# An eight-batch linear attention and gMLP kernel on one core: a product in one bank of a PSUM pair no longer waits for an addition that reads the other bank, and the order of all steps is searched anew

## The chip, the cores and the metric

The kernel runs on one core of a Trainium2 chip. The metric is the time of the whole program on the device, in microseconds (us). The engines that matter are TensorE (PE, matrix products into PSUM), VectorE (DVE), ScalarE (ACT), GpSimd (POOL) and the queues that move data between memory and the chip.

## The reference

```python
# 8 batches, 8 heads, S = 576 positions, head size 64, model size 512
q_s = softmax(q, over the head's 64)          # 1e-9 added to each sum
k_s = softmax(k, over the 576 positions)
kv  = einsum('bhsd,bhse->bhde', k_s, v)
x   = einsum('bhsd,bhde->bhse', q_s, kv)      # then 576 x 512 per batch

h    = gelu_tanh(x @ w_in)                    # 576 x 1024
u, v = h[..., :512], h[..., 512:]
v_n  = (v - mean(v)) / sqrt(var(v) + 1e-6) * g_ln
v_s  = einsum('ts,bsd->btd', w_sg, v_n) + b_sg
out  = x + (u * v_s) @ w_out
```

All is float32.

## The kernel before, in words

**Products.** Each float32 product is made of three faster ones: an operand is cast to a reduced form `hi` (on ACT), the rest `lo` = operand − `hi` is formed by a subtraction (on DVE or POOL), and PE adds up hi·hi, hi·lo and lo·hi. A step that makes such a `lo` thus stands between the value and a third of its products.

**Steps of a batch b.** `load_q`, `load_k`, `load_v`; the two softmaxes (`q_…`, `k_…`); `kv_mm`; `x_mm`, which gives x, kept as `x_h` and `x_l`; the v half of the first layer (`hv_mm`, 12 matmuls of 512 columns for each of five row blocks, GELU, and the statistics and scaling of the layernorm); the u half (`hu_mm`, 24 matmuls of 288 columns for each quarter); `sg_mm`, the product with w_sg; `gate`, u·v_s, in place of u; then the product with w_out, and `out_store`. The steps of three batches or so are interleaved, so that PE works on one batch while DVE, ACT and POOL prepare another.

**The last product in batches 2 to 7.** It is made by a scheme of seven products in place of eight: after the `gate` steps, `t_1` to `t_4` subtract quarters of u from each other in place; for each of seven operands m, `p_high b m` and `p_low b m` make hi and lo; and `out_p b t m` is the product m for output half t (0 or 1), six matmuls of 288 columns. Sums of products are formed in PSUM as far as they can be, and the rest is added into the output tiles `o`, which `out_base` has set to x. In batches 0 and 1 the product is plain (`out_mm`, `out_add`).

**PSUM.** `ps2` is three tiles of two banks each, `ps1` two tiles of one bank; `bank()` deals them in turn. All seven products of (b, t) go into one pair: bank 0 takes m = 1, 6, 5, 3 and bank 1 takes m = 2, 7, 4. Products 1, 2 and 7 start a bank afresh, the other four go on adding to what is there. DVE reads a pair between the products: `o_p1` reads bank 0 after product 1, `o_p2` bank 1 after product 2, `o_u2` both banks after products 6 and 7, `o_u4` bank 0 after product 5, `o_p3` bank 0 after product 3, `o_p4` bank 1 after product 4.

**What sets the order.** `PLAN` is a text of 1404 steps; the letter V, A or G at a step gives its engine (DVE, ACT, POOL). The steps are issued in that order. The class `InOrder` ties each instruction of SP, DVE, ACT and POOL to the one before it on its engine, and `mm` keeps PE's in program order, so that each engine works off its steps in the text's order, and an engine whose next step waits does nothing else. Between engines, the framework that places the waits follows tiles: a step that reads a PSUM pair waits for every product issued into that pair before it, and a product waits for every earlier reader of the pair, whichever bank each of them touches.

In the profile all instructions of DVE, ACT, POOL and SP carry the line of `InOrder`'s call (L176 before, L175 in the changed kernel), and all matmuls that of `mm` (L276, L275). In the rows, `o<-ps,o` is one of the additions into the output, `lo<-u,hi` is `p_low` or its like in batches 0 and 1, `u<-u` and `u<-u,u` are `t_1` to `t_4`, `ps<-hi,wo_h` (or `lo,wo_h` or `hi,wo_l`) are matmuls of the last product, `ps<-wi_h,x_h` begins an `hv_mm`, and `ps<-qt,kvt` is `x_mm`.

Of the kernel before, what the change touches and what calls it, by code (L numbers as in the profile page):

```python
# [50 lines left out]
load_w_in 4, neg, load_k 1 0, wi_l 1 G, wi_l 0 G, wi_a 2, kv_scale 0 1, wi_b 2, xf_mm 0 0 1, xf_high 0 0 1, wi_a 4, xf_neg 0 0 1, xf_low 0 0 1 A
load_q 1 1, warm 0, xf_mm 0 1 0, q_swapm 1 0, wi_c 2, xf_mm 0 1 1, wi_d 2, wi_h 3, wi_x 3, load_w_sg 4, k_ma 1 0, wi_h 2, wi_l 2 G, load_k 1 1
xf_high 0 1 0, xf_neg 0 1 0, wi_l 3 A, wi_b 4, k_mb 1 0, k_mc 1 0, kt_mm 1 0, wi_c 4, q_max 1 1, k_top 1 0, xf_high 0 1 1, xf_low 0 1 0 A
hu_part 0 2 0, wi_d 4, q_swapm 1 1, load_w_in 6, kb_mm 1 0, k_ma 1 1, q_top 1 1, wi_h 4, q_top 1 0, hu_gpart 0 2 0, load_w_sg 0, xf_low 0 1 1
# [4 lines left out]
wi_l 4 G, hu_gpart 0 1 1, q_mul 1 0 1 G, q_turn 1 1, kb_mm 1 1, hv_mm 0 0, k_sub 1 1 V, hu_gpart 0 2 1, q_sum 1 1, wo_a 3, wo_a 2, wo_a 1, b_l G
hu_part 0 3 1, hv_gelu 0 0 A, g_safe, wo_a 0, wo_b 0, wo_b 1, wo_c 1, wo_z 3, hv_sq 0 0, hu_gpart 0 3 1, q_swapd 1 1, wo_b 3 A, q_inv 1 1, hv_mm 0 3  # L60
hv_gelu 0 3 A, hu_gpart 0 3 0, load_v 1 0, hv_sq 0 3, wo_b 2, kv_mm 1 0, q_mul 1 1 1 G, kv_inv 1 0, kv_scale 1 0, q_mul 1 1 0 V, x_mm 1 0
hv_stat 0 0 A, hv_mm 0 1, load_w_sg 1, q_turn 1 2, hv_pow 0 0, k_exp 1 1, q_turn 1 3, x_high 1 1, wo_c 0, wo_d 0, x_high 1 0, x_low 1 0, hv_gelu 0 1 A
hv_sq 0 1, wo_d 3, hv_stat 0 3 A, hv_pow 0 3, load_v 1 1, kv_mm 1 1, kv_inv 1 1, kv_scale 1 1, x_neg 1 1, x_mm 1 1, x_low 1 1 A, hv_stat 0 1 A
hv_cen 0 0 A, wo_c 2, x_high 1 3, wo_d 1, load_w_sg 2, hv_pow 0 1, x_high 1 2, hv_cen 0 3 A, x_low 1 3, hv_high 0 0, hv_cen 0 1 A, x_low 1 2, wo_d 2
hv_low 0 0 V, ws_l 0 V, hv_high 0 3, g_rows, hv_low 0 3 V, hv_mm 0 2, hv_gelu 0 2, hv_stat 0 2, load_q 2 0, hv_high 0 1, hv_low 0 1 V, hv_mm 0 4
hv_gelu 0 4 A, hv_sq 0 4, hv_pow 0 2, ws_h 1, ws_l 4 G, wo_h 2, hv_mm 1 3, hv_gelu 1 3 A, hv_sq 1 3, hv_stat 0 4 A, hv_cen 0 2 A, hv_pow 0 4
# [1112 lines left out]
```

## Time and profile before

| | |
|---|---|
| time, median of 3 runs | 503.99 us (503.92, 503.99, 504.9) |
| the profiled execution | 505.95 us, of which 504.2 us is the span of the trace |
| granted TensorE clock, mean over the span | 0.996 |
| busy: PE, DVE, ACT, POOL | 477.0, 371.7, 302.9, 211.4 us |
| chain that ended last: PE, DVE, DMA | 79%, 13%, 3% of the span |
| mean rate of memory traffic | 95 GB/s |

The span is the time from the first to the last instruction of the trace. The profiled execution lies 1.96 us above the median of the timed ones. An engine's idle time in a row, such as `[0.91 <-DVE o L176]`, is the time that it stood still ahead of the instruction, and the arrow names what released it. Consecutive matmuls overlap in their records: one begins before the record of the last has ended.

### The profile page before, as it was taken

Reading aid. Unit: us, or ns where it says so; the run is one execution under the profiler, and the core shown is the slowest. Engines: PE = TensorE matmul, PEld = TensorE weight load, DVE = VectorE, ACT = ScalarE, POOL = GpSimd, SP = SyncE. Lnnn points to the kernel's source line nnn. Section 1 sums busy time; section 2 is a strip of 40 time slices with the busy share of each in tenths; the row PEclk is TensorE's granted clock in tenths of the full one; section 3 lists DMA queues with packets and bytes.
Section 4 is the critical chain, followed back from the end, with each engine's and each line's share of the span. In section 5 each row is a group of like instructions: output and inputs, shape, how many; then the busy total and the mean of one; then the engine's idle time right before and its main releaser. Section 6 shows DMA issues by size and latency. Waiting matters only on the chain.

```text
span 504.2 us, 9419 instructions
## 1 busy us (share of the span) xinstructions
PE 477.0 (95%) x3775; PEld 436.3 (87%) x3775; DVE 371.7 (74%) x658; ACT 302.9 (60%) x571; POOL 211.4 (42%) x165
## 2 busy tenths in 40 slices
PE   3899899999999999989999999999997999999986
PEld 3778689998998899878998889988996889979985
DVE  5999978896988796696798967786887453544155
ACT  5999997584473785656756775485434653254121
POOL 5436232745325256753346154482044510235221
PEclk9999999999999999999999999999998999999999
DMA  8894330028104700037003620036201210002002
GB/s 305 328 385 181 79 146 1 1 65 283 54 7 134 258 2 2 0 107 290 4 1 106 213 81 1 1 107 211 82 2 54 78 72 1 0 1 95 0 2 94
DMA packets 16611, 48.32 MB, mean 96 GB/s; under 512 B 3508, under 2 KB 3640, under 8 KB 16568
## 3 DMA queue, kind: packets, MB, share of 16 engines
q1 hardware_dynamic: 16416, 47.66, 26.9%
q8 instruction: 29, 0.48, 0.4%
q14 instruction: 14, 0.11, 0.1%
q10 hardware_dynamic: 152, 0.07, 0.0%
HBM read 38.28 MB, written 9.44 MB: 95 GB/s over the span
## 4 chain that ended last, share of the span: by engine, by line
PE 79%; DVE 13%; DMA 3%; issue 2%; ACT 1%; SPq 1%; POOL 1%; ACTq 0%
PE ps L276 79%; DVE ot_i L176 2%; DVE o L176 2%; DMA kqk<-k 2%; DVE km L176 1%; DVE qd L176 1%; DMA kqq<-q_flat 1%; SPq L176 1%; DVE qm L176 1%; DVE qt L176 1%; DVE lo L176 1%; DVE kqk L176 1%; DVE kqq L176 0%; DVE x_l L176 0%; ACT u L176 0%
## 5 line engine op out<-in xcount | busy, mean ns | idle before, releaser
L176 ACT CAST hi<-u 128x576 fp32r<-128x576 f32 x46 | 30.7, 672 | 65.6 <-DVE u L176 32.0
L276 PE MATMUL ps<-hi,wo_h 128*128 128x288 f32 x200 | 58.7, 307 | 7.4 <-DVE o L176 6.6
L176 DVE TENSOR_TENSOR o<-ps,o 128x288 f32<-128x288 f32 (+1 forms) x80 | 41.0, 525 | 26.9 <-PE ps L276 26.7
L276 PE MATMUL ps<-lo,wo_h 128*128 128x288 f32 x200 | 57.1, 299 | 2.3 <-DVE lo L176 2.2
L176 POOL TENSOR_TENSOR rs<-ve,half 128x1 f32<-128x1 f32 x36 | 25.9, 723 | 79.6 <-DVE ve L176 78.5
L276 PE MATMUL ps<-hi,wo_l 128*128 128x288 f32 x200 | 57.0, 298 | 0.0
L276 PE MATMUL ps<-ws_h,vnh 128*128 128x288 f32 x256 | 54.8, 295 | 0.1
L276 PE MATMUL ps<-ws_h,vnl 128*128 128x288 f32 x256 | 54.6, 294 | 0.0
L276 PE MATMUL ps<-ws_l,vnh 128*128 128x288 f32 x256 | 54.6, 294 | 0.0
L176 POOL TENSOR_TENSOR lo<-u,hi 128x576 fp32r<-128x576 f32 x21 | 33.4, 1595 | 48.0 <-ACT hi L176 47.9
L176 ACT ACTIVATE v<-v,nb,rs 128x512 f32<-128x512 f32 x36 | 29.2, 816 | 35.0 <-DVE nb L176 27.6
L276 PEld LDWEIGHTS ps<-hi,wo_h 128*128 128x128 f32 x200 | 37.2, 190 | 11.9 <-DVE o L176 5.7
L176 POOL TENSOR_TENSOR vnl<-v,vnh 128x512 fp32r<-128x512 f32 x20 | 29.0, 1457 | 42.8 <-ACT vnh L176 40.1
L176 DVE SCALAR_TENSOR_TENSOR u<-ps,gp,u 128x576 f32<-128x576 f32 x32 | 25.6, 809 | 26.1 <-PE ps L276 25.8
L176 ACT ACT_TABLE_LOAD x32 | 41.1, 1283 | 2.6 <-issue 2.0
L276 PEld LDWEIGHTS ps<-ws_h,vnh 128*128 128x128 f32 x256 | 41.1, 188 | 0.9 <-ACT u L176 0.4
L276 PE MATMUL ps<-x_h,wi_h 128*128 128x288 f32 (+2 forms) x256 | 40.9, 300 | 0.7 <-ACT u L176 0.4
L276 PEld LDWEIGHTS ps<-ws_l,vnh 128*128 128x128 f32 x256 | 41.0, 188 | 0.0
L276 PEld LDWEIGHTS ps<-ws_h,vnl 128*128 128x128 f32 x256 | 41.0, 188 | 0.0
L276 PE MATMUL ps<-wi_h,x_h 128*128 128x512 f32 x144 | 40.3, 402 | 0.1
L276 PE MATMUL ps<-x_h,wi_l 128*128 128x288 f32 (+2 forms) x256 | 40.1, 297 | 0.1
L276 PEld LDWEIGHTS ps<-lo,wo_h 128*128 128x128 f32 x200 | 37.2, 190 | 3.5 <-DVE lo L176 3.0
(171 smaller groups left out, 1195.3 us busy)
## 6 DMA issues: line engine op xcount, KB each, us to landing
out<-o SPq DMA_DIRECT2D x32, 288.0 KB, 2.8
kqk<-k SPq DMA_DIRECT2D x14, 640.0 KB, 7.6
kqq<-q SPq DMA_DIRECT2D x14, 576.0 KB, 4.8
kqv<-v SPq DMA_DIRECT2D x12, 650.0 KB, 3.9
x_lk<-k_turn SPq DMA_DIRECT2D x4, 288.0 KB, 5.5
raw_i_vnl<-w_in SPq DMA_DIRECT2D x2, 512.0 KB, 5.7
raw_i_vnh<-w_in SPq DMA_DIRECT2D x2, 512.0 KB, 8.3
raw_i_wo_h<-w_in SPq DMA_DIRECT2D x2, 512.0 KB, 7.3
```

What stands on the lines that cost most here:

```text
L176: ins = op(*args, **kw)
L276: tc.keep_in_program_order(nc.tensor.matmul(*args, **kw))
```

## The change

Two things are changed. First, the products and additions on a PSUM pair are noted with the bank that they use (`apart`), and for each product and addition of *different* banks of the pair the framework is told that one need not wait for the other. `o_u2`, which reads both banks, is left as it was. Second, `PLAN` is another order of the same 1404 steps, with other engine letters at about a hundred of them: 58 steps go from DVE to POOL (among them 12 `p_low`, 9 `hv_low`, 8 `q_mul`, 6 `out_base`, 2 `t_4`) and 48 from POOL to DVE (10 `p_low`, 7 `hv_low`, 6 `q_mul`, 5 `out_base`). The arithmetic is the same; PE has the same number of matmuls.

```diff
 PLAN = """
-hv_gelu 6 3 A, o_p1 5 0, o_p1 5 1, q_mul 7 1 1 V, out_p 5 1 2, hv_sq 6 3, hv_mm 6 2, t_3 5 G, p_low 5 6 G, out_p 5 1 6, p_high 5 7, out_p 5 0 6
+out_p 5 1 1, out_p 5 1 2, k_rotb 7, t_2 5 G, t_4 5 V, t_3 5 G, out_p 5 0 2, hv_mm 6 3, q_turn 7 1, p_high 5 6, p_high 5 7, o_p1 5 0, o_p1 5 1
...
     def mm(*args, **kw):
-        tc.keep_in_program_order(nc.tensor.matmul(*args, **kw))
+        ins = nc.tensor.matmul(*args, **kw)
+        tc.keep_in_program_order(ins)
+        return ins.ins
...
         for i, (l, r) in enumerate(pairs):
-            mm(to, l, r, start=fresh and i == 0, stop=i == len(pairs) - 1, skip_group_check=not fresh)
+            apart(b, t, 0 if m in (1, 6, 5, 3) else 1, "mm", mm(to, l, r, start=fresh and i == 0, stop=i == len(pairs) - 1, skip_group_check=not fresh))
...
-    def into(z, ps):
-        V.tensor_tensor(out=z, in0=ps, in1=z, op=ALU.add)
+    banks = {}
+
+    def apart(b, t, n, kind, ins):
+
+        log = banks.setdefault(id(st["o", b, t]), [])
+        for m, other, earlier in log:
+            if m != n and other != kind:
+                tc.declare_no_dep(ins, earlier, reason="another PSUM bank")
+        log.append((n, kind, ins))
+        del log[:-80]
+
+    def into(b, t, z, n):
+        ps = st["o", b, t]
+        ins = V.tensor_tensor(out=z, in0=ps[:, :, 0:HS] if n is None else ps[:, n, 0:HS], in1=z, op=ALU.add)
+        if n is not None:
+            apart(b, t, n, "sum", ins.ins)
 
     def o_p1(b, t):
-        into(o_of(b, t)[:, FIRST], st["o", b, t][:, 0, 0:HS])
+        into(b, t, o_of(b, t)[:, FIRST], 0)
...
     def o_u2(b, t):
-        into(split(o_of(b, t + 2)), st["o", b, t][:, :, 0:HS])
+        into(b, t, split(o_of(b, t + 2)), None)
```

What moves is seen at three places. The first is DVE in the middle of batch 5's last product. `o5_0` and `o5_1` are the output tiles of the halves t = 0 and 1, `ps2_2` and `ps2_0` their PSUM pairs, `ve6`, `mv6` and `s66` the layernorm statistics of batch 6, `qt7`, `kqq_7` and `km7` softmax work of batch 7. Before:

```order
L176 TENSOR_TENSOR o5_0_4138<-ps2_2_79,o5_0_4138 128x288
L176 TENSOR_TENSOR o5_1_4177<-ps2_0_77,o5_1_4177 128x288
L176 TENSOR_TENSOR kqq_7_1_3901<-kqq_7_1_3901,qd7_4014 128x576
L176 STREAM_TRANSPOSE qt7_0_4175<-kqq_7_0_3875 128x576
L176 BN_STATS s66_1_4292<-v6_1_4244 128x6
L176 BN_AGGR mv6_1_4293<-s66_1_4292 128x2
L176 TENSOR_SCALAR ve6_1_4296<-mv6_1_4293 128x1
L176 STREAM_TRANSPOSE km7_0_4180<-km7_0_4180 128x256
L176 TENSOR_REDUCE kf7_4183<-km7_0_4180 128x8
L176 TENSOR_TENSOR o5_0_4138<-ps2_2_79,o5_0_4138 128x288
```

In the changed kernel, from the first addition of batch 5 to the fourth:

```order
L175 TENSOR_TENSOR o5_0_4203<-ps2_2_79,o5_0_4203 128x288
L175 TENSOR_TENSOR o5_1_4032<-ps2_0_77,o5_1_4032 128x288
L175 STREAM_TRANSPOSE qt7_0_4270<-kqq_7_0_3924 128x576
L175 TENSOR_TENSOR o5_1_4032<-x_h5_3244,x_l5_3254 128x576
L175 TENSOR_TENSOR o5_1_4032<-ps2_0_77,o5_1_4032 128x288
L175 TENSOR_TENSOR kf7_4141<-kf7_4141,kb7_4244 128x16
L175 STREAM_TRANSPOSE km7_1_4103<-kf7_4141 128x256
L175 TENSOR_TENSOR o5_0_4203<-ps2_2_79,o5_0_4203 128x288
```

Between the first two additions and the next of DVE there were seven other instructions, and now there are two; the second addition of half 1 comes ahead of that of half 0, and the subtraction `p_low 5 7`, which stood four rows behind the last one shown before, is POOL's now.

The second is PE where the attention product `x_mm 1 0` of batch 1 stands among the `hv_mm` of batch 0. `kqk_1` are the exponentials of k, `qt1` and `kvt1` the operands of `x_mm`. Before:

```order
L276 MATMUL ps1_0_80<-wi_h_61,x_h0_260 128x512 x4
L276 MATMUL ps1_0_80<-wi_h_61,x_l0_290 128x512 x4
L276 MATMUL ps1_0_80<-wi_l_62,x_h0_260 128x512 x4
L276 MATMUL ps1_1_81<-raw_i_wo_h_87,kqk_1_0_295 64x65 x20
L276 MATMUL ps2_2_79<-qt1_0_510,kvt1_0_636 64x288 x2
L276 MATMUL ps2_0_77<-qt1_0_510,kvt1_0_636 64x288 x2
L276 MATMUL ps2_2_79<-qt1_0_510,kvt1_0_636 64x288 x2
L276 MATMUL ps2_0_77<-qt1_0_510,kvt1_0_636 64x288 x2
L276 MATMUL ps1_0_80<-wi_h_61,x_h0_260 128x512 x4
```

In the changed kernel:

```order
L275 MATMUL ps1_1_81<-raw_i_wo_h_87,kqk_1_0_304 64x65 x20
L275 MATMUL ps1_0_80<-wi_h_61,x_h0_291 128x512 x4
L275 MATMUL ps1_0_80<-wi_h_61,x_l0_307 128x512 x4
L275 MATMUL ps1_0_80<-wi_l_62,x_h0_291 128x512 x4
L275 MATMUL ps2_2_79<-qt1_0_617,kvt1_0_635 64x288 x2
L275 MATMUL ps2_0_77<-qt1_0_617,kvt1_0_635 64x288 x2
L275 MATMUL ps2_2_79<-qt1_0_617,kvt1_0_635 64x288 x2
L275 MATMUL ps2_0_77<-qt1_0_617,kvt1_0_635 64x288 x2
```

An `hv_mm` of twelve matmuls that was ahead of `kv_mm` (the row of twenty matmuls) now stands between `kv_mm` and `x_mm`.

The third is PE a little earlier, where the maxima of k of batch 1 (`km1_1`, `kt1_1`) are turned by products with the identity `eye`. Before:

```order
L276 MATMUL ps1_1_81<-eye_72,km1_1_378 128x128 x2
L276 MATMUL ps2_1_78<-eye_72 128x128 x2
L276 MATMUL ps2_2_79<-eye_72 128x128 x2
L276 MATMUL ps2_0_77<-eye_72 128x128 x2
L276 MATMUL ps2_1_78<-x_h0_260,wi_h_61 128x320 x4
...
L276 MATMUL ps2_0_77<-x_l0_290,wi_h_61 128x320 x4
L276 MATMUL ps1_0_80<-eye_72,kt1_1_467 128x128 x2
L276 MATMUL ps1_1_81<-wi_h_61,x_h0_260 128x512 x4
```

In the changed kernel:

```order
L275 MATMUL ps2_0_77<-x_l0_307,wi_h_61 128x320 x4
L275 MATMUL ps1_1_81<-eye_72,km1_1_431 128x128 x2
L275 MATMUL ps1_0_80<-eye_72,kt1_1_509 128x128 x2
L275 MATMUL ps1_1_81<-wi_h_61,x_h0_291 128x512 x4
L275 MATMUL ps1_0_80<-wi_h_61,x_h0_291 128x512 x4
```

Between the two there were products of the u half for PE to do, and now the second, which needs what DVE makes of the first, follows it at once.

## Rows read from the trace of the kernel before

**Rows 1.** Page, part 1: busy us, share of the span, instructions by engine.

```profile
PE 477.0 (95%) x3775; PEld 436.3 (87%) x3775; DVE 371.7 (74%) x658; ACT 302.9 (60%) x571; POOL 211.4 (42%) x165
```

**Rows 2.** Page, part 4: the chain that ended last, by engine.

```profile
PE 79%; DVE 13%; DMA 3%; issue 2%; ACT 1%; SPq 1%; POOL 1%; ACTq 0%
```

**Rows 3.** Waits of PE from 203 to 486 us: us in total, times, longest.

```profile
PE ps L276 <- DVE o L176: 5.1, 8, 0.9
PE ps L276 <- DVE lo L176: 2.2, 2, 1.1
PE ps L276 <- DVE ve L176: 0.6, 1, 0.6
```

**Rows 4.** Timeline, batch 5: start, us, engine, line, operation [idle before <-releaser].

```profile
378.71 0.82 DVE L176 TENSOR_TENSOR o<-ps,o 128x288 f32<-128x288 f32 x2 [1.49 <-PE ps L276]
...
379.59 0.40 PE L276 MATMUL ps<-hi,wo_h 128*128 128x288 f32 x1 [0.91 <-DVE o L176]
...
384.61 0.30 PE L276 MATMUL ps<-lo,wo_h 128*128 128x288 f32 x1
...
384.75 0.29 PE L276 MATMUL ps<-hi,wo_l 128*128 128x288 f32 x1
385.08 0.46 DVE L176 TENSOR_TENSOR o<-ps,o 128x288 f32<-128x288 f32 x1 [2.11 <-PE ps L276]
...
385.68 0.37 PE L276 MATMUL ps<-hi,wo_h 128*128 128x288 f32 x1 [0.64 <-DVE ve L176]
...
386.33 0.71 DVE L176 TENSOR_TENSOR lo<-u,hi 128x576 fp32r<-128x576 f32 x1
...
387.10 0.40 PE L276 MATMUL ps<-lo,wo_h 128*128 128x288 f32 x1 [1.04 <-DVE lo L176]
```

**Rows 5.** Timeline of PE, 215 to 228 us.

```profile
217.59 0.40 PE L276 MATMUL ps<-hi,wo_h 128*128 128x288 f32 x1 [0.27 <-DVE o L176]
...
219.69 0.37 PE L276 MATMUL ps<-hi,wo_h 128*128 128x288 f32 x1 [0.25 <-DVE o L176]
...
226.41 0.40 PE L276 MATMUL ps<-hi,wo_h 128*128 128x288 f32 x1 [0.92 <-DVE o L176]
```

**Rows 6.** Windows, PE: stretch, us, PE busy (matmuls), granted clock, DMA share, GB/s.

```profile
387.00:391.00 4.00, 3.90 (x15) 0.57 0.00 2
```

**Rows 7.** Timeline, startup, PE, then DVE.

```profile
42.75 1.18 PE L276 MATMUL ps<-wi_h,x_h 128*128 128x512 f32 x4
...
54.14 1.20 PE L276 MATMUL ps<-qt,kvt 64*64 64x288 f32 x16 [1.44 <-DVE kvt L176]
...
61.58 1.20 PE L276 MATMUL ps<-wi_h,x_h 128*128 128x512 f32 x4
...
41.70 2.05 DVE L176 TENSOR_TENSOR wi_l<-ot_i,wi_h 128x512 fp32r<-128x512 f32 x2
```

**Rows 8.** Timeline, the tail.

```profile
487.92 0.76 DVE L176 TENSOR_TENSOR lo<-u,hi 128x576 fp32r<-128x576 f32 x1
...
489.19 0.38 PE L276 MATMUL ps<-hi,wo_h 128*128 128x288 f32 x1 [1.27 <-DVE o L176]
...
492.06 0.40 PE L276 MATMUL ps<-hi,wo_h 128*128 128x288 f32 x1 [0.25 <-DVE o L176]
```

**Rows 9.** Groups by line: operation, xcount, busy us, mean ns, idle before.

```profile
L176 POOL TENSOR_TENSOR lo<-u,hi 128x576 fp32r<-128x576 f32 x21 | 33.4, 1595 | 48.0 <-ACT hi L176 47.9
...
L176 DVE TENSOR_TENSOR lo<-u,hi 128x576 fp32r<-128x576 f32 x25 | 20.5, 825 | 9.9 <-ACT hi L176 9.9
```

**Rows 10.** Timeline, POOL and DVE at the same time, batch 5.

```profile
322.13 0.76 DVE L176 TENSOR_TENSOR u<-u,u 128x576 f32<-128x576 f32 x1
...
373.97 1.97 POOL L176 TENSOR_TENSOR lo<-u,hi 128x576 fp32r<-128x576 f32 x1 [3.54 <-ACT hi L176]
...
374.56 1.99 DVE L176 TENSOR_TENSOR u<-u,u 128x576 f32<-128x576 f32 x1
```

More of the change, by code (lines that the diff above doesn't have):

```diff
@@ L51 @@
[L51 to L54, printed above, removed]
@@ L59 @@
[L59 to L62, printed above, removed]
@@ L63 @@
[L63 to L66, printed above, removed]
@@ L95 @@
-sg_mm 2 1, gate 2 1, sg_mm 2 3, s_l 3, p_high 2 1, p_low 2 1 G, out_p 2 0 1, hv_cen 3 1 A, t_1 2 V, p_high 2 5, k_fold 4 0, p_low 2 5 V, k_rota 4
-gate 2 3, out_p 2 1 1, tail_high 3, p_high 2 2, q_mul 4 1 1 G, k_maxa 4, t_2 2 G, p_high 2 6, t_3 2 V, p_low 2 2 V, hv_mm 3 0, p_low 2 6 G, o_p1 2 1
-out_p 2 0 2, out_p 2 1 2, hv_stat 3 3 A, p_high 2 7, o_p1 2 0, k_rotb 4, out_p 2 0 6, o_p2 2 0, o_p2 2 1, p_low 2 7 V, tail_low 3, out_base 2 3 G
-out_p 2 1 6, k_maxb 4, hv_high 3 1, hv_low 3 1 G, q_turn 4 2, q_turn 4 3, tail_again 3, out_p 2 0 7, out_p 2 1 7, o_u2 2 1, o_u2 2 0, p_high 2 3
@@ L111 @@
-out_base 3 3 V, hv_mm 4 3, o_p1 3 1, p_low 3 6 G, out_p 3 1 6, o_p2 3 1, o_p1 3 0, o_p2 3 0, p_high 3 7, p_low 3 7 G, k_wide 5 0, out_p 3 1 7
-out_p 3 0 6, out_p 3 0 7, o_u2 3 1, o_u2 3 0, out_p 3 1 5, hv_sq 4 1, hv_stat 4 1 A, hv_gelu 4 3, k_exp 5 1, k_sub 5 0 G, load_v 5 1, hv_stat 4 3
-o_u4 3 1, out_p 3 0 5, p_high 3 3, k_exp 5 0, hv_pow 4 1, t_4 3 V, hv_pow 4 3, load_v 5 0, hv_stat 4 0 A, hv_pow 4 0, p_high 3 4, kv_mm 5 1, kv_mm 5 0
-p_low 3 4 V, load_q 6 1, load_q 6 0, out_p 3 1 4, kv_inv 5 1, hv_cen 4 1 A, out_p 3 0 4, kv_inv 5 0, hv_cen 4 3 A, hv_cen 4 0 A, p_low 3 3 V
@@ L123 @@
-hv_cen 5 2 A, out_p 4 0 1, gate 4 3, hu_mm 5 1, p_low 4 5 G, t_2 4 V, t_3 4 V, q_mul 6 0 0 G, p_high 4 2, out_p 4 1 1, o_p1 4 0, hv_pow 5 0, k_rotb 6
-p_low 4 2 G, tail_high 5, out_p 4 1 2, hv_cen 5 0 A, hv_high 5 0, q_turn 6 2, p_high 4 6, out_p 4 0 2, hv_mm 5 3, p_high 4 7, k_maxb 6, tail_low 5
-p_low 4 6 V, hv_high 5 2, p_low 4 7 G, q_turn 6 3, k_wide 6 1, o_p1 4 1, o_p2 4 1, o_p2 4 0, out_p 4 1 6, out_p 4 0 6, out_p 4 0 7, out_p 4 1 7
-k_sub 6 1 G, hv_mm 5 1, q_turn 6 0, hv_gelu 5 3 A, hv_sq 5 3, k_wide 6 0, k_exp 6 1, k_sub 6 0 V, o_u2 4 0, o_u2 4 1, out_p 4 0 5, load_v 6 0, t_4 4 G
@@ L135 @@
-out_p 5 1 1, q_mul 7 1 0 G, k_mc 7 0, p_low 5 2 G, q_mul 7 0 1 V, hv_mm 6 3, t_2 5 V, p_high 5 6, out_base 5 3 V, out_p 5 0 2, hv_gelu 6 1
-hv_gelu 6 3 A, o_p1 5 0, o_p1 5 1, q_mul 7 1 1 V, out_p 5 1 2, hv_sq 6 3, hv_mm 6 2, t_3 5 G, p_low 5 6 G, out_p 5 1 6, p_high 5 7, out_p 5 0 6
-q_turn 7 1, hv_stat 6 1, hv_pow 6 1, out_base 5 2 G, k_fold 7 0, o_p2 5 0, hv_stat 6 3 A, hv_cen 6 1 A, q_turn 7 3, p_low 5 7 V, o_p2 5 1, hv_high 6 1
-t_4 5 V, hv_gelu 6 2, out_p 5 0 7, k_rota 7, k_maxa 7, k_rotb 7, out_p 5 1 7, o_u2 5 1, hv_mm 6 0, hv_low 6 1 G, hv_gelu 6 0, k_maxb 7, o_u2 5 0
@@ L147 @@
-gate 6 2, p_high 6 2, out_p 6 1 1, t_2 6 V, p_high 6 6, p_low 6 2 V, hv_mm 7 1, o_p1 6 1, t_3 6 G, hv_gelu 7 1 A, out_p 6 0 2, o_p1 6 0, p_low 6 6 V
-out_p 6 1 6, out_p 6 0 6, out_p 6 1 2, o_p2 6 0, hv_mm 7 0, o_p2 6 1, p_high 6 7, hv_sq 7 1, p_low 6 7 V, out_p 6 0 7, tail_high 7, tail_again 7
-out_base 6 2 G, out_p 6 1 7, hv_stat 7 1 A, p_high 6 3, tail_low 7, hv_pow 7 1, o_u2 6 1, hv_gelu 7 0 A, hv_sq 7 0, hv_high 7 3, p_low 6 3 G
-hv_cen 7 1 A, hv_mm 7 2, o_u2 6 0, out_p 6 0 5, t_4 6 V, o_u4 6 0, out_p 6 1 5, p_high 6 4, p_low 6 4 G, hv_high 7 1, hv_low 7 1 V, out_p 6 0 3
@@ L155 @@
[L155 to L158 removed]
+load_b A, load_q 0 1 1, load_eye A, warm 4, load_q 0 0 0, load_k 0 0 0, qf_max 0 0 0, qf_sub 0 0 0 G, kr_zero 0 1, b_h, qf_exp 0 0 0, qf_max 0 1 1
@@ new lines @@
+p_low 2 5 G, t_2 2 V, t_3 2 V, o_p1 2 0, q_mul 4 1 0 G, p_low 2 2 V, out_p 2 0 2, p_high 2 6, p_low 2 6 V, o_p2 2 0, out_p 2 1 2, k_rotb 4, p_high 2 7
+load_v 4 0, out_p 2 0 6, hv_pow 3 1, tail_high 3, o_p1 2 1, hv_pow 3 3, hv_cen 3 3 A, t_4 2 G, out_p 2 1 6, o_p2 2 1, tail_again 3, k_maxb 4
+p_low 2 7 V, k_wide 4 1, out_p 2 1 7, out_p 2 0 7, hv_cen 3 1 A, tail_low 3, q_turn 4 3, o_u2 2 1, k_sub 4 1 G, k_wide 4 0, hv_mm 3 2, o_u2 2 0
+p_high 2 3, p_low 2 3 V, hv_high 3 3, k_sub 4 0 V, hv_gelu 3 0 A, hv_sq 3 0, hv_stat 3 0 A, hv_low 3 3 G, q_turn 4 2, out_p 2 1 5, out_p 2 0 5
@@ new lines @@
+out_p 3 1 6, k_exp 5 1, out_p 3 0 6, p_high 3 3, o_u2 3 1, load_v 5 0, out_p 3 0 7, o_u2 3 0, out_p 3 1 5, o_u4 3 1, out_p 3 0 5, kv_mm 5 0
+p_high 3 4, p_low 3 3 V, load_v 5 1, p_low 3 4 G, load_q 6 1, hv_stat 4 3, kv_inv 5 0, kv_scale 5 0, hv_pow 4 3, hv_cen 4 3 A, kv_mm 5 1, out_p 3 1 4
+kv_inv 5 1, load_q 6 0, out_p 3 0 4, out_p 3 1 3, o_u4 3 0, o_p4 3 1, out_store 3 3, load_k 6 1, o_p3 3 1, hv_cen 4 0 A, o_p4 3 0, out_p 3 0 3
+kv_scale 5 1, xm_mm 5, xm_high 5 0, xt_high 5, out_store 3 2, q_max 6 1, o_p3 3 0, xm_low 5 0, hv_high 4 0, hu_mm 4 1, xt_low 5, hv_mm 4 4
@@ new lines @@
+p_low 5 6 G, out_p 5 0 6, out_p 5 1 6, q_turn 7 0, out_base 5 3 V, hv_pow 6 1, o_p2 5 1, hv_mm 6 2, k_maxb 7, q_mul 7 1 1 G, k_wide 7 1, p_low 5 7 G
+o_p2 5 0, out_p 5 0 7, hv_cen 6 1 A, q_turn 7 3, out_base 5 2 G, load_v 7 0, hv_gelu 6 3 A, out_p 5 1 7, k_wide 7 0, k_sub 7 0 V, o_u2 5 0, o_u2 5 1
+hv_sq 6 3, hv_stat 6 3 A, hv_mm 6 0, p_high 5 3, p_low 5 3 G, out_p 5 1 5, out_p 5 0 5, hv_gelu 6 2, hv_stat 6 2, hv_pow 6 2, hv_high 6 1, o_u4 5 0
+hv_low 6 1 G, hv_gelu 6 0, hv_stat 6 0, hv_pow 6 0, hu_mm 6 0, o_u4 5 1, p_high 5 4, out_p 5 0 3, hv_pow 6 3, out_p 5 1 3, p_low 5 4 V, out_p 5 0 4
@@ new lines @@
+hv_stat 7 1 A, o_p2 6 0, out_p 6 0 7, out_base 6 3 G, o_u2 6 0, o_u2 6 1, hv_high 7 3, hv_pow 7 1, p_high 6 3, hv_gelu 7 0 A, hv_sq 7 0, t_4 6 V
+hv_mm 7 2, hv_stat 7 0 A, hv_low 7 3 G, out_p 6 0 5, out_p 6 1 5, o_u4 6 1, tail_again 7, hu_mm 7 2, o_u4 6 0, hv_gelu 7 2, p_high 6 4, p_low 6 3 G
+out_p 6 0 3, o_p3 6 0, out_store 6 0, hv_cen 7 1 A, out_p 6 1 3, o_p3 6 1, p_low 6 4 G, out_p 6 0 4, hv_pow 7 0, hv_cen 7 0 A, o_p4 6 0, hv_high 7 0
+hv_high 7 1, hv_stat 7 2, hv_pow 7 2, hv_low 7 0 G, out_p 6 1 4, hu_mm 7 1, hu_gelu 7 2, o_p4 6 1, hv_cen 7 2 A, out_store 6 2, hv_high 7 2
@@ new lines @@
+hu_gelu 7 1, hv_low 7 1 G, hu_mm 7 0, hv_low 7 2 V, sg_mm 7 0, sg_mm 7 1, gate 7 1, hu_gelu 7 0, gate 7 0, t_1 7 V, out_store 6 1, out_base 7 0 V
+sg_mm 7 3, out_store 6 3, out_base 7 2 G, out_base 7 1 V, p_high 7 5, hu_mm 7 3, out_base 7 3 G, hu_gelu 7 3, p_high 7 1, gate 7 3, p_low 7 5 V
+p_low 7 1 V, sg_mm 7 2, gate 7 2, out_p 7 0 1, p_high 7 2, t_2 7 V, out_p 7 1 1, p_low 7 2 V, out_p 7 0 2, p_high 7 6, o_p1 7 0, p_low 7 6 V
+out_p 7 1 2, out_p 7 0 6, t_3 7 V, p_high 7 7, o_p1 7 1, o_p2 7 0, p_low 7 7 V, out_p 7 1 6, o_p2 7 1, out_p 7 0 7, o_u2 7 0, out_p 7 1 7, o_u2 7 1
@@ L159 @@
+out_p 7 0 5, o_u4 7 0, p_high 7 3, out_p 7 1 5, o_u4 7 1, p_low 7 3 G, out_p 7 0 3, out_p 7 1 3, o_p3 7 0, t_4 7 G, p_high 7 4, p_low 7 4 V
+out_p 7 0 4, o_p3 7 1, out_store 7 0, out_p 7 1 4, o_p4 7 0, out_store 7 1, out_store 7 2, o_p4 7 1, out_store 7 3
 """
```

183 lines of the change are left out of this document (95 added, 88 removed).

## The prediction

> **What bounds the kernel now.** I read the busy times first: PE is busy 477.0 of 504.2 us, the next engine, DVE, 371.7 [rows 1]. The chain that ended last says the same: 79% of it is PE, 13% DVE [rows 2]. The number of matmuls is not changed, so the time can fall by no more than what PE stands still or runs slowly: the question is which of these stretches the change takes away, and which it makes.
>
> So next the waits of PE. From 203 us, where batch 2's last product is near, to 486 us, where only batch 7's is left, three rows hold them: on `o`, on `lo` and on `ve` [rows 3]. Then the timeline, to see what kind of wait each is. Batch 5 shows them all [rows 4]. The matmul at 379.59 is product 2 of half 1. It starts bank 1 afresh, which nobody has yet read, but waits 0.91 for the additions at 378.71, which read bank 0. The addition at 385.08 is `o_p2 5 0`. It reads bank 1 after product 2, done at about 378.7, yet DVE stands still 2.11 us until the matmul of 384.75, the last of product 6 in bank 0, has ended. Behind it in DVE's queue wait the layernorm's small steps and the subtraction at 386.33, `p_low 5 7`, and PE waits for both: 0.64 at 385.68 (product 7 of half 0 may not start before `o_p2` has read its bank: a true wait, but on an addition held up by a false one; the name in the row, `ve`, is DVE's next instruction) and 1.04 at 387.10, where the second matmul of product 7 wants its `lo`. So the price is not the wait between banks alone; most of it is what queues behind.
>
> **The false waits, 203 to 486 us.** The three rows sum to 5.1 + 2.2 + 0.6 = 7.9 us in 11 waits [rows 3]. Two of them are true ones, an addition of the same bank that comes late: 0.27 at 217.59 and 0.25 at 219.69 [rows 5]; 0.92 at 226.41 is a false one again (product 4, bank 1, against an addition of bank 0). That leaves 7.4 us in 9 waits: two of `lo`, one of `ve`, six of `o`. An idle time in a row is less than what the wait costs. Matmuls of 288 columns follow one another so closely that each record of 0.30 overlaps the next by 0.16 (384.61 + 0.30 − 384.75), and the first after a wait takes 0.40, 0.10 more [rows 4]. So 7.4 + 9 × 0.26 = 9.7 us.
>
> To it comes the clock. From 387 to 391 us PE was granted 0.57 of its full clock, that is mostly 1.2 GHz in place of 2.4 [rows 6]; this follows on the three waits of batch 5 named above. 4.0 × 0.43 = 1.7 us. If the waits go, I expect this to go with them; that is not certain, and if it stays, 1.7 us come back. Together −11.4 us.
>
> **The start.** In its first 60 us the kernel waits for DVE, and here the new order counts, not the banks. `x_mm 1 0` waits 1.44 at 54.14 for `kvt` [rows 7]. In the new order an `hv_mm` stands ahead of it, 2.8 us of PE's time. DVE's work up to `kvt` is as long as before by my count of its instructions, so PE, which was there at 52.7, comes at 55.5, later than `kvt`, and the wait goes: 1.44 + 0.26 = 1.7. Against it, the transposition of `kt1_1` now follows directly on that of `km1_1`, and DVE makes the first from the second behind two `wi_l` subtractions (2.05 us for two, at 41.70) that stood behind it before. PE must wait here some 1.5 to 2.4 us; but the u-half products that filled this gap are now done ahead of it, so that the `hv_mm` which began at 42.75 begins at about the same time, 42 to 44. The next landmark, the `hv_mm` at 61.58, then comes 59.8 to 60.4. I take −1.5, with −3 and +1.5 as ends (both waits gone; the wait on the transposition twice as long with nothing won back).
>
> **The tail.** Batch 7 has nothing beside it. There product 2 of half 1 waits 1.27 at 489.19 for an addition of the other bank; its own `lo` is ready at 488.68 (487.92 + 0.76) [rows 8]. So 489.19 − 488.68 = 0.5 us go here, and 0.25 + 0.26 = 0.5 at 492.06, where a product waits for an addition that itself waited for the other bank. `p_low 7 4`, still on DVE behind an addition, gives back 0.1 by my count of DVE's rows. So −0.9, with 0 and −2 as ends (both eaten up by DVE's queue; the whole 1.27 and both overlaps gone).
>
> **What is new and may wait.** 58 steps go from DVE to POOL and 48 the other way; twelve `p_low` are among the 58. The same subtraction takes 825 ns on DVE and 1595 ns on POOL [rows 9]. Where the step lies ahead of its product by more than this, it costs nothing; PE's work of the next batch stands between most of them, as the 2.8 us of an `hv_mm`. Batch 5 has its subtractions 6, 7 and 3 on POOL one behind the other; `p_low 5 7` is no longer behind an addition, and its longer time is the price. The trace of before does not show the new queue. From below, no new wait: 0. From above, a wait at each product of a longer `lo`. By the nearest row, the true wait at 219.69 with 0.25 + 0.26 = 0.5 us [rows 5], and one or two in each of six batches, it is 3 to 6. I take 3.0, one for each batch.
>
> One row speaks against steps on POOL. The DVE subtraction at 374.56 takes 1.99 us where the same took 0.76 at 322.13; beside it POOL works from 373.97 to 375.94, and it ends 0.61 after POOL does [rows 10]: it seems to have stood still until POOL was done. The Trainium skill has this as a rule (SBUF — State Buffer, "Who interferes with whom"): a DVE instruction with two inputs in SBUF and a GpSimd instruction that reads SBUF want the same read port, and whoever comes first keeps the other out until it is done. The trace agrees, 1.99 against 0.76. By the rule each such meeting would cost DVE up to a whole POOL instruction, not a share of it.
>
> **The sum.** −1.5 − 11.4 − 0.9 + 3.0 = −10.8 us on the profiled execution's own 505.95 us: 495.15. That execution lies 1.96 above the median of the runs, so for the median 503.99 − 10.8 = 493.2 us.
>
> **Rivals.**
>
> *R1: half is given back.* The false waits go, but they had also given DVE, POOL and the loads time; when products come sooner, `lo` and the inputs of later batches are late instead. For it: `lo` is what PE waits for in two of the eleven rows' waits [rows 3]. Against it: DVE has 132 us idle and POOL 293 [rows 1]. The new waits are then 8 in place of 3: 498.2.
>
> *R2: the waits stay.* An addition may still come late because DVE's queue, in order, holds it behind others, or a product because `o_u2`, which is not exempted, reads both banks. Then only the order's other effects are left, start and tail against the new waits: −1.5 − 0.9 + 3.0 = +0.6, 504.6 us. Against it: in batch 5 only two rows stand between DVE's additions where seven stood, and each of the additions 1 and 2 follows its own product.
>
> *R3: slower, by POOL.* The 58 moved steps come late, since POOL takes 1.595 − 0.825 = 0.77 longer for each, and PE, first in 79% of the chain, waits. What is won is 1.5 + 11.4 + 0.9 = 13.8, so it decides from 13.8 / 0.77 = 18 of the 58 on. With 25 of them it is 503.99 − 13.8 + 19.3 = 509.5. By the price of a blocked DVE instruction in rows 10, 1.99 − 0.76 = 1.23 each, 11 would do. For it: rows 10. Against it: POOL is busy 42% of the span, and 48 steps come the other way.
>
> **How the numbers follow.** The forecast 0.68, R1 0.22, R2 0.04, R3 0.06. A measurement of this kernel can tell 0.2%, 1.0 us, from no change. The forecast's own range is 489.5 to 496.5. Its best case is −3 − 11.4 − 2 + 0 = −16.4, 487.6, its worst +1.5 − 11.4 + 0 + 6 = −3.9, 500.1; with R1 the range is 488.5 to 500.0. Outside it are R2, R3 and the ends of both. Faster (under 503.0): the forecast and R1 and a little of R2, 0.91; same (503.0 to 505.0): most of R2, 0.03; slower: R3, 0.06.
>
> **What would show it.** PE's waits on `o` between 203 and 486 us fall from 5.1 us to under 1.5, and no product follows on an addition of the other bank. DVE's idle ahead of `o<-ps,o`, 2.11 at its longest in batch 5, no longer has a product of the other bank as its releaser. The granted clock does not fall around 387. `x_mm 1 0` has no wait, and a wait of 1.5 to 2.4 us stands after the transposition of `km1_1`. If PE waits on `lo` in sum for over 5 us, made by POOL, it is R1 or R3; if waits on `o` of 0.6 to 0.9 are there still, R2. A loss of clock elsewhere (1.7 us a time) or a start later by more than 1.5 us would make my sum wrong without touching the mechanism.

## The result, and the profile after

The changed kernel took 492.98 us (median of 4, 492.5 to 493.29) against 503.96 (4 runs): ratio 0.9778, 95% interval 0.9761 to 0.9795. The forecast was 493.2. The profiled execution took 492.82 us, with a span of 491.0 and the full clock throughout.

The busy times and the chain of the changed kernel, to be set against [rows 1, 2]:

```profile
PE 473.0 (96%) x3775; PEld 434.9 (89%) x3775; DVE 359.4 (73%) x647; ACT 297.4 (61%) x567; POOL 221.9 (45%) x176
...
PE 71%; DVE 15%; DMA 6%; issue 3%; POOL 2%; ACT 2%; DVEq 0%; SPq 0%; POOLq 0%
```

PE's part of the chain falls from 79% to 71%. Between the first 57 us, in which DVE and the loads decide, and the tail the chain leaves PE four times, for 77 us in all, and each time it comes back at a wait of PE (146.03, 214.56, 233.62 and 343.00 us). These four waits come with the new order and are treated below; the version there that has the old order behind the start has 80%. PE's busy time falls by 4.0 us for the same 3775 matmuls. 2.5 of them are missing in a second profile of the kernel before as well (474.5 us, the control below), in which the clock did not fall; the first record after each wait is longer, too.

PE's waits from 203 to 486 us, to be set against [rows 3] (us in total, times, longest):

```profile
PE ps L275 <- DVE o L175: 1.4, 2, 0.9
PE ps L275 <- DVE vnl L175: 0.9, 1, 0.9
PE ps L275 <- DVE lo L175: 0.7, 2, 0.4
```

They fell from 7.9 us in 11 waits to 3.0 in 5. (The stretch is fixed in time, and in the changed kernel it takes in most of batch 7's last product, where both waits on `lo` stand. Up to there it is 2.3 us in 3.) Batch 5, which held five of the nine false waits, has none left. Its additions on DVE, where [rows 4] showed 1.49 and 2.11 us of standing still, and two matmuls of PE beside them:

```profile
374.13 0.78 DVE L175 TENSOR_TENSOR o<-ps,o 128x288 f32<-128x288 f32 x2
...
376.14 0.30 PE L275 MATMUL ps<-hi,wo_h 128*128 128x288 f32 x1
...
376.16 0.45 DVE L175 TENSOR_TENSOR o<-ps,o 128x288 f32<-128x288 f32 x1
...
376.81 0.30 PE L275 MATMUL ps<-hi,wo_l 128*128 128x288 f32 x1
...
377.69 0.42 DVE L175 TENSOR_TENSOR o<-ps,o 128x288 f32<-128x288 f32 x1
...
381.31 1.41 DVE L175 TENSOR_TENSOR o<-ps,o 128x576 f32<-128x576 f32 x2
```

The first four additions run without an idle time ahead of them. The product that each of them reads had ended before DVE's turn came, and the `hv_mm` between the products covers DVE's time. The third addition, `o_p2 5 1` at 376.16, shows the change itself: it reads bank 1 while PE, from 376.14 to 377.1, makes product 6 in bank 0 of the same pair (the first and the last of its six matmuls are shown). The clock in that stretch, to be set against [rows 6] (us, PE busy, granted clock, DMA share, GB/s):

```profile
380.00:394.00 14.00, 14.00 (x99) 1.00 0.34 128
```

At the start and in the tail (timeline of PE, to be set against [rows 7, 8]):

```profile
41.01 0.43 PE L275 MATMUL ps<-eye,kt 128*128 128x128 f32 x2 [1.24 <-DVE kt L175]
41.20 1.18 PE L275 MATMUL ps<-wi_h,x_h 128*128 128x512 f32 x4
...
53.10 1.20 PE L275 MATMUL ps<-qt,kvt 64*64 64x288 f32 x16
...
57.00 1.20 PE L275 MATMUL ps<-qt,kvt 64*64 64x288 f32 x16 [1.38 <-DVE kvt L175]
...
58.50 1.10 PE L275 MATMUL ps<-wi_h,x_h 128*128 128x512 f32 x4
...
473.90 0.29 PE L275 MATMUL ps<-hi,wo_h 128*128 128x288 f32 x1
...
476.47 0.40 PE L275 MATMUL ps<-lo,wo_h 128*128 128x288 f32 x1 [0.39 <-DVE lo L175]
...
485.60 0.40 PE L275 MATMUL ps<-lo,wo_h 128*128 128x288 f32 x1 [0.30 <-DVE lo L175]
```

`x_mm 1 0`, at 53.10, waits no longer; `x_mm 1 1`, at 57.00, now waits 1.38 for `kvt`. The foreseen wait for `kt` is there with 1.24. In the tail the waits for additions are gone, and two short ones for `lo` are left.

**Where the time came from.** For a comparison I use a second profile of the kernel before (the control below), since the first one had lost 1.7 us to the clock and waited 1.0 us longer for its first load (5.85 against 4.81). Four landmarks in it, and in the changed kernel (timeline of PE; the `hv_mm` of [rows 7], the first product of batch 2, the first of batch 7, PE's last matmul):

```profile
61.16 1.20 PE L276 MATMUL ps<-wi_h,x_h 128*128 128x512 f32 x4
...
202.49 0.30 PE L276 MATMUL ps<-hi,wo_h 128*128 128x288 f32 x1
...
483.79 0.30 PE L276 MATMUL ps<-hi,wo_h 128*128 128x288 f32 x1
...
497.81 0.29 PE L276 MATMUL ps<-hi,wo_l 128*128 128x288 f32 x1
```

```profile
201.47 0.29 PE L275 MATMUL ps<-hi,wo_h 128*128 128x288 f32 x1
...
487.03 0.29 PE L275 MATMUL ps<-hi,wo_l 128*128 128x288 f32 x1
```

With 58.50 and 473.90 from above, the stretches are:

| stretch | before | changed | difference | forecast |
|---|---|---|---|---|
| to the `hv_mm` | 61.16 | 58.50 | −2.7 | −1.5 |
| to batch 2's products | 141.33 | 142.97 | +1.6 | (in the +3.0) |
| to batch 7's products | 281.30 | 272.43 | −8.9 | −11.4 + 3.0 |
| tail | 14.02 | 13.13 | −0.9 | −0.9 |
| sum | 497.81 | 487.03 | −10.8 | −10.8 |

The +1.6 in the second row can't be put down to the new order: the first profile of the kernel before has 142.4 in this stretch, and the old order without the waits (below) 142.7. The two profiles of the kernel before differ here by 1.0 us.

### The profile page after: what moved, and what is told of

The parts are those of the page before. It is cut to its first block, busy times and chain, and to the rows that moved or that the text cites. A ratio compares the mean times of both kernels' runs of the same rounds, so it can differ in the third digit from the quotient of the medians.

```text
span 491.0 us, 9420 instructions
## 1 busy us (share of the span) xinstructions
PE 473.0 (96%) x3775; PEld 434.9 (89%) x3775; DVE 359.4 (73%) x647; ACT 297.4 (61%) x567; POOL 221.9 (45%) x176
## 4 chain that ended last, share of the span: by engine, by line
PE 71%; DVE 15%; DMA 6%; issue 3%; POOL 2%; ACT 2%; DVEq 0%; SPq 0%; POOLq 0%
PE ps L275 71%; DMA kqq<-q 3%; DVE ot_i L175 2%; DVE km L175 2%; DVE u L175 2%; DMA x_lv<-v 2%; DVE o L175 1%; DMA raw_i_vnl<-w_in 1%; DVE lo L175 1%; DVE vn L175 1%; DVE qd L175 1%; DVE qm L175 1%; ACT hi L175 1%; DVE x_l L175 1%; DMA kqq<-q_flat 1%
## 5 line engine op out<-in xcount | busy, mean ns | idle before, releaser
L175 POOL TENSOR_TENSOR lo<-u,hi 128x576 fp32r<-128x576 f32 x22 | 31.8, 1450 | 74.0 <-ACT hi L175 47.6
L275 PE MATMUL ps<-hi,wo_h 128*128 128x288 f32 x200 | 57.2, 299 | 1.2 <-DVE o L175 0.9
L175 POOL TENSOR_TENSOR rs<-ve,half 128x1 f32<-128x1 f32 x36 | 27.5, 770 | 42.5 <-DVE ve L175 42.5
L175 POOL TENSOR_TENSOR vnl<-v,vnh 128x512 fp32r<-128x512 f32 x22 | 30.2, 1377 | 25.2 <-ACT vnh L175 25.2
L175 POOL TENSOR_TENSOR kqq<-kqq,qd 128x576 f32<-128x576 f32 (+2 forms) x19 | 24.6, 1302 | 37.0 <-DVE qd L175 27.2
L275 PE MATMUL ps<-x_l,wi_h 128*128 128x288 f32 (+2 forms) x256 | 39.8, 295 | 0.0
```

The costliest lines, as they stand in the source:

```text
L175: ins = op(*args, **kw)
L275: ins = nc.tensor.matmul(*args, **kw)
```

## The experiments

The kernels of one group ran on the same chip beside the same runs of the kernel before. Ratios are to those.

### The two halves of the change, and a control

The kernel before, unchanged:

> The kernel before, unchanged, profiled a second time. The first profiled execution took 505.95 us, 2.0 over the median. If the fall of the clock at 387 us belonged to that execution, the second shows a full clock there and a time near 504.0, and the 1.7 us of the clock were no part of what the change gained in the median. If the fall belongs to the three waits ahead of it, it is there again. The wait for the first load (5.9 us before, 4.6 after) tells in the same way whether 1.2 us at the start were the load's chance.

It took 503.6 us. The three rows of waits of [rows 3] came again (5.1, 2.2 and 0.6 us), but the clock did not fall (windows, columns as above):

```profile
386.00:391.00 5.00, 4.72 (x26) 1.00 0.01 2
```

In the kernel with the new start below, which has the same waits, the clock fell again, to 0.70 in this stretch. The same waits are thus followed by a fall in some executions and not in others. The profiles of the changed kernel and of the old order without the waits have none here.

How often the kernel before loses clock can be read from its other runs, each of which has its mean granted clock on record; the profile with the fall has 0.996, the control 0.999. Of the 19 runs that stood beside this control nine have 0.996 or 0.997 and ten 0.999 or 1.000; on the chips of the two later groups it is 8 of 11 and 4 of 10. So a loss of this size is in 21 of 40 executions, and not a thing of the first profile alone. The medians of the runs with it and of those without are 505.07 and 504.02 us here, 505.88 and 504.11, 505.81 and 503.38 on the other two chips: 1.1 to 2.4 us apart. Where in these runs the clock was lost is not known, since the trace of the profiled one alone was kept.

The old order without the waits (the edit is against the changed kernel; of a long one, here and below, a line or two is shown):

```diff
 PLAN = """
-load_b A, load_q 0 1 1, load_eye A, warm 4, load_q 0 0 0, load_k 0 0 0, qf_max 0 0 0, qf_sub 0 0 0 G, kr_zero 0 1, b_h, qf_exp 0 0 0, qf_max 0 1 1
...
+out_p 5 0 2, hv_gelu 6 1, hv_gelu 6 3 A, o_p1 5 0, o_p1 5 1, q_mul 7 1 1 V, out_p 5 1 2, hv_sq 6 3, hv_mm 6 2, t_3 5 G, p_low 5 6 G
...
```

> Order and engine letters of before, with the waits between banks taken away. Theory 1 (the false waits were the price, and mostly what queues behind them): nine waits with their overlap, 9.7 us, and 1.0 at the tail go, less a little for true waits that show up: 493.5 to 496. Theory 2 (an order searched with the false waits in it can't use their absence, the new order is what gains): less than half goes, 499 to 503.

Measured: 491.99 us against 504.85, ratio 0.9746 (0.9726 to 0.9766). Theory 1 holds, and by more than it said. Of PE's waits from 203 to 486 us one is left, in the tail; between the first product of batch 2 and the first of batch 7 there is none, and these two landmarks are 269.9 us apart, where the control had 281.3:

```profile
PE ps L284 <- DVE lo L184: 0.4, 1, 0.4
...
203.98 0.30 PE L284 MATMUL ps<-hi,wo_h 128*128 128x288 f32 x1
...
473.84 0.30 PE L284 MATMUL ps<-hi,wo_h 128*128 128x288 f32 x1
```

The new order without the exemption (`into`, `apart` and `mm` as before):

```diff
-            apart(b, t, 0 if m in (1, 6, 5, 3) else 1, "mm", mm(to, l, r, start=fresh and i == 0, stop=i == len(pairs) - 1, skip_group_check=not fresh))
+            mm(to, l, r, start=fresh and i == 0, stop=i == len(pairs) - 1, skip_group_check=not fresh)
```

> The new order and letters, with the waits between banks left as before. Theory 1: the new order puts products of the other bank ahead of the additions more freely, so that there are at least as many false waits as before, and only the start's 1.5 to 3 us are gained: 502 to 512. Theory 2: most of the gain is the order's, 494 to 499.

Measured: 503.32 us, ratio 0.9973 (0.9954 to 0.9991), inside theory 1's range. PE's waits on `o` from 203 to 486 us are even longer than before:

```profile
PE ps L284 <- DVE o L184: 7.0, 8, 1.4
```

The whole gain of the change is thus the exemption's; the new order by itself brings 0.3%.

The new order up to the `hv_mm` at 61.6 us alone, the rest as before:

> The kernel before with the new order of the steps up to the hv_mm at 61.6 us alone, no wait taken away. By my count of the start 1.5 us are gained: 502.0 to 502.8. If the 3.2 us by which the profile of after is ahead there are all the order's, 500.8; if they were the first load's chance for the most part, 503.5 to 504.

Measured: 502.55 us, ratio 0.9954 (0.9935 to 0.9974), 2.3 us less than its own before of 504.85: between the 1.5 and the 3.2 of the two first cases. The start is a true gain of the order.

### Which of the two directions costs

Two kernels with the old order and half of the exemption each. Only additions freed, then (with `kind == "mm"`) only products:

```diff
-            if m != n and other != kind:
+            if m != n and other != kind and kind == "sum":
```

> Old order; only the additions are freed: an addition does not wait for a product of the other bank, but a product still waits for an addition of the other bank. If the price lies in DVE's queue (an addition held up, and the lo subtraction and the next additions behind it), an early addition is over before the product comes, and nearly all of the gain is there: 492 to 494.5. If it lies in the products' own wait, 497 to 501.

> Old order; only the products are freed: a product does not wait for an addition of the other bank, but an addition still waits for the products of the other bank that stand ahead of it. By the rows of before the six waits on o go with their overlap (4.6 + 6 x 0.26 = 6.1 us, and 0.5 to 1.5 in the tail), and the two on lo and the one behind the held-up addition stay (2.8 + 0.8 = 3.6): 497 to 499. If the products' own wait is all of it, 492 to 493.

Measured against 505.59 us: additions free 495.28, ratio 0.9803 (0.9784 to 0.9822), 10.3 us; products free 499.22, ratio 0.989 (0.9866 to 0.9913), 6.4 us. In microseconds both lie a little above their ranges, 492 to 494.5 and 497 to 499; but this group's runs of the kernel before are 1.6 us slower than the 503.99 that the ranges were worked out from, and with that taken off both are inside. Waits of PE from 203 to 486 us, with the additions free, then with the products free:

```profile
PE ps L284 <- DVE o L184: 3.1, 4, 1.3
```

```profile
PE ps L284 <- DVE lo L184: 3.1, 4, 1.1
PE ps L284 <- DVE o L184: 1.4, 3, 0.6
PE ps L284 <- DVE ve L184: 0.6, 1, 0.6
```

With additions free all waits on `lo` and `ve` go and some on `o` remain (the longest, 1.27, in the tail). With products free both long waits on `lo` remain (1.04 and 1.14), and two shorter ones are new (0.57, and 0.39 in the tail). The two halves sum to more than the whole (10.3 + 6.4 against 2.54% of 505, 12.8), since a wait of PE on an addition that is itself held up goes in both, as those of 0.91 do that stand at 211.87 and 379.59 in the kernel before. The larger price lay in DVE's queue, as the reading of batch 5 had it.

### What the rest of the new order costs

New start, old order and letters from there, with the exemption; and the changed kernel again beside it:

```diff
...
-s1_c V, hv_low 1 1 G, sg_mm 1 0, gate 1 0, s3_a G, q_swapm 3, sg_mm 1 3, out_base 1 3 G, xm_low 2 1, q_top 3, gate 1 3, gate_high 1 0, gate_low 1 0 V
...
+out_p 5 0 2, hv_gelu 6 1, hv_gelu 6 3 A, o_p1 5 0, o_p1 5 1, q_mul 7 1 1 V, out_p 5 1 2, hv_sq 6 3, hv_mm 6 2, t_3 5 G, p_low 5 6 G
...
```

> The new order up to the hv_mm at 61.6 us, the old order from there, the waits between banks taken away. If the gains add up, the order of before with no such waits (0.9746 of before) and the new start (0.9954 of before) make 0.970, that is 489.0 to 490.5 for a before of 504.9. If the lead of the start is given back at the next step that waits for a load or for DVE, as the kernel with the new start alone gave back some 2 us between 62 and 203 us, 491 to 493.

> The changed kernel unchanged, on the chip and beside the runs of before that the three others share, to set it against the old order without the waits. That one came to 0.9746 of before where the changed kernel had 0.9778. If the new order costs 1 to 2 us, 0.9778 comes again while the kernel with the new start and the old rest lies under 0.974; if the two are equal, this lies at 0.975 to 0.976.

Measured against 505.59 us: 490.3, ratio 0.9704 (0.9685 to 0.9722), and the changed kernel 494.0, ratio 0.9789 (0.9762 to 0.9815). The gains of exemption and new start add up (0.9746 × 0.9954 = 0.970), and this version beats both kernels. It shares its start with the changed kernel, so what the latter loses lies behind 62 us. In the profiles it is 491.0 − 488.1 = 2.9 us of span. The four landmarks in this version:

```profile
58.67 1.09 PE L284 MATMUL ps<-wi_h,x_h 128*128 128x512 f32 x4
...
201.35 0.29 PE L284 MATMUL ps<-hi,wo_h 128*128 128x288 f32 x1
...
471.04 0.29 PE L284 MATMUL ps<-hi,wo_h 128*128 128x288 f32 x1
...
484.11 0.29 PE L284 MATMUL ps<-hi,wo_l 128*128 128x288 f32 x1
```

The changed kernel is 0.3 us longer from the `hv_mm` to batch 2's products, 2.7 from there to batch 7's, and the same in the tail. Four waits of PE that the old order does not have account for it: one in the first of these stretches, where the old order has three short ones of its own (0.30, 0.21 and 0.16), and three in the second, with 0.89 + 0.86 + 0.52 and 0.26 of overlap each 3.0 us. Two of the four, with what POOL and DVE did ahead of them (timeline of the changed kernel):

```profile
143.81 0.67 ACT L175 CAST hi<-u 128x576 fp32r<-128x576 f32 x1 [2.62 <-DVE u L175]
...
144.56 1.41 POOL L175 TENSOR_TENSOR lo<-u,hi 128x576 fp32r<-128x576 f32 x1 [0.88 <-ACT hi L175]
...
146.03 0.54 PE L275 MATMUL ps<-lo,wo_h 128*128 128x288 f32 x2 [0.86 <-POOL lo L175]
...
209.54 0.19 PEld L275 LDWEIGHTS ps<-lo,wo_h 128*128 128x128 f32 x1
...
209.59 3.47 DVE L175 TENSOR_TENSOR vn<-v,vn 64x512 fp32r<-64x512 f32 x1
...
214.56 0.40 PE L275 MATMUL ps<-hi,wo_h 128*128 128x288 f32 x1 [0.89 <-DVE o L175]
```

At 146.03 PE waits for `gate_low 1 1`, which the new letters put on POOL: its hi is done at 144.48, and POOL takes 1.41. At 214.56 the cause stands five us earlier: POOL's `k_sub 4 1` (`kqk`, on DVE before) begins at 209.54, DVE's subtraction for the layernorm 0.05 later, and it takes 3.47 us. It ends 0.56 after POOL does, and the additions behind it are late. The other two are 0.86 at 233.62, for a `vnl` that stands in DVE's queue behind a maximum of q whose load came late (in one of two profiles), and 0.52 at 343.00, where an `hu_mm` waits for batch 4's additions to free its PSUM pair.

Whether POOL's instruction was the cause, by one letter (the steps stand here in the lines of the changed kernel):

```diff
-p_low 2 7 V, k_wide 4 1, out_p 2 1 7, out_p 2 0 7, hv_cen 3 1 A, tail_low 3, q_turn 4 3, o_u2 2 1, k_sub 4 1 G, k_wide 4 0, hv_mm 3 2, o_u2 2 0
+p_low 2 7 V, k_wide 4 1, out_p 2 1 7, out_p 2 0 7, hv_cen 3 1 A, tail_low 3, q_turn 4 3, o_u2 2 1, k_sub 4 1 V, k_wide 4 0, hv_mm 3 2, o_u2 2 0
```

> The changed kernel with one letter changed: k_sub 4 1 on DVE in place of POOL. In the changed kernel it ran on POOL from 209.54 to 212.50, and DVE's subtraction tail_low 3 beside it took 3.47 us in place of 0.69, so that o_u2 2 1 was late and PE waited 0.89 (0.89 + 0.16 more in all) at 214.56. If POOL's instruction holds DVE's, tail_low 3 takes 0.7, this wait goes or shrinks under 0.3, and PE gains about 1 us on its way to the next step that waits. If it is DVE's queue by itself (its length was the cause, and the 3.47 a record's error), the wait is there as before or is longer by k_sub's 1.5 us on DVE.

Timeline of DVE:

```profile
211.91 0.69 DVE L184 TENSOR_TENSOR vn<-v,vn 64x512 fp32r<-64x512 f32 x1
...
213.33 0.72 DVE L184 TENSOR_TENSOR o<-ps,o 128x576 f32<-128x576 f32 x1
213.97 1.47 DVE L184 TENSOR_TENSOR kqk<-kqk,km 128x1280 f32<-128x1280 f32 x1
```

The subtraction takes 0.69, and no wait of PE stands before batch 2's product 5, although DVE now does `k_sub` itself (1.47 where POOL took 2.96). The time, 490.43 us against 504.19, ratio 0.9734 (0.9696 to 0.9772), does not stand clear of the changed kernel's 0.9789 (0.9762 to 0.9815); that the wait is gone is shown, that the whole gets 1 us faster is not.

### Engine letters by themselves

The version with the new start and the old order behind it, with the new letters at 98 steps of the rest (two of them shown, each on a line of its own), and the changed kernel with the old letters at 106:

```diff
-k_sub 2 0 V
-k_sub 2 1 V
+k_sub 2 0 G
+k_sub 2 1 G
...
```

> New start, old order of the rest, no waits between banks, but with the engine letters of the changed kernel at the 98 steps of the rest where they differ (some 50 go from DVE to POOL). If steps on POOL come late at 0.77 us each (my rival that ended slower), PE's waits on lo and on o rise and it loses much: with 10 of them late 7.7 us, 498. If the letters are nearly free, 490 to 492 like the kernel with the old letters (490.3); a meeting of a long POOL instruction with a DVE subtraction here and there costs about 1 us each.

> The changed kernel's order with the engine letters of before at all 106 steps where they differ, no waits between banks. The changed kernel (0.9789 of before) loses 0.85% against new start with old rest (0.9704). If the letters are what it loses by, this one lies at 490 to 492; if the order, 494 to 496; letters and order were searched together, so that it may also be worse than both, above 496.

Measured against 504.19 us: 522.04, ratio 1.0354 (1.0325 to 1.0384), and 526.41, ratio 1.0436 (1.0409 to 1.0464). Both lie far above every figure that was given; only "worse than both, above 496", for the second, has no upper end. Letters of one order on the other cost some 32 us either way. Waits of PE, over the whole span, and the clock, of the first:

```profile
PE ps L284 <- POOL lo L184: 7.9, 5, 2.8
PE ps L284 <- ACT kqk L184: 6.7, 5, 3.5
PE ps L284 <- DVE lo L184: 5.4, 6, 2.2
...
core 0: 520.2 us, clock 0.984
```

Waits on `lo` and `kqk` are 20.0 us in 16, where the version with the old letters has 0.7 in 2. The clock of 0.984 stands for some 0.016 × 520 = 8.3 us more, an estimate. One of these places (timeline, POOL and PE):

```profile
112.69 6.20 POOL L184 TENSOR_TENSOR kqk<-kqk,km 128x1280 f32<-128x1280 f32 x2
...
116.94 1.63 PE L284 MATMUL ps<-kqv,kqk 128*64 128x65 f32 x40 [3.48 <-ACT kqk L184]
```

Two `k_sub` one behind the other on POOL take 6.2 us, and `kv_mm` of batch 2 waits 3.48 for the exponentials behind the first.

## Why the prediction was right, and where only in sum

**The false waits: right in mechanism, and in size by luck.** The nine waits are gone, and the half with the additions freed shows that what queues behind an addition is the larger part. But the term −11.4 was made of 9.7 for waits and 1.7 for the clock, and the waits alone were worth 281.3 − 269.9 = 11.4, between two profiles in which the clock did not fall here. The waits of the control in this stretch, each with 0.26 of overlap, make up just that. The nine give 9.7. The two at 217.59 and 219.69, which I had left out as true waits that stay, give 1.0; they went too, because those additions were late for the same reason, DVE's queue: with only the additions freed both are gone, with only the products freed both are there (0.54 and 0.24). One of 0.34 on `x_l` at 355.28, which the first profile does not have, gives 0.6. The clock should not have been taken off whole from the median: about half of the executions of the kernel before lose it, and the others do not. So a right total came from two errors of opposite sign.

**The start: right place, too small.** −2.7 against −1.5. The `hv_mm` ahead of `x_mm 1 0` took its wait away as worked out, and the wait for `kt` was 1.24, under the 1.5 to 2.4 taken; the `hv_mm` behind it, expected at 42 to 44, began at 41.20. The wait of `x_mm 1 1` grew from 0.33 to 1.38, which I had not seen.

**The tail: right,** −0.9.

**New waits: right in sum, not in place.** 3.0 was taken. Against the old order with the same start the rest of the new order costs 2.9 us of span, in four waits. I had put one of 0.5 in the last product of each of six batches; one came there (214.56), one in batch 1's, one at an `sg_mm`, and one at an `hu_mm` that needs a PSUM pair of batch 4 (343.00).

**The rivals.** R2 fell with the first profile: waits on `o` from 5.1 to 1.4 us. R1, half given back, is not what happened: the version with the new start and the old order behind it gained 497.81 − 484.11 = 13.7 us on the control, and the changed kernel 10.8, so that 2.9 were given back where R1 had 8. R3, slower by POOL, did not happen to this kernel, but its mechanism is there: of the four new waits one is a `lo` on POOL and one a DVE subtraction that stood still beside POOL. The latter is the rule of the Trainium skill cited in the prediction (SBUF — State Buffer, "Who interferes with whom"); the trace agrees, with 3.47 in place of 0.69, and at the change of one letter 0.69. That there are only two is probably because order and letters were found together; with the letters of the other order the loss was 32 us, above the 19.3 that I had priced for 25 late steps.

**What stays open.** Why the clock falls after the same waits in some executions only. (The Trainium skill, TensorE: Matmul & The Clock Gate, "Part 1: The HAM clock gate (the "warmup" mystery)", says that the point at which the clock rises at a kernel's start varies from run to run. That is another place than this one: here the clock fell in the middle of the kernel, in two of three profiles.) By the medians the changed kernel lies 3.7 us above the best version, by the profiles 2.9. Part of this is the clock again: its runs at 1.000 have a median of 492.82, 2.5 above the 490.3 of the other, all of whose runs are at 1.000; two of the remaining three are at 0.995, with 495.48 and 496.55, and the third, 494.87 at 0.999, is not explained.

## What to carry to other kernels

Where two engines share a tile of several PSUM banks, look for waits whose releaser worked in a bank that the waiting instruction does not touch, and price them with what queues behind on the in-order engine. When an order and an assignment to engines were found together, do not put one of them whole on another partner; a single letter can still be changed, if the trace says which. And when a change consists of a new freedom and a new order, run the old order with the freedom too: here it had the whole gain. Before a loss of clock that one profile shows is taken off a median, look at the clock of the timed runs: here about half of them had it.
